# Batch 6's keys and queries turned by DMA, and divisions and roundings on any engine

## The chip, the core and the metric

The kernel runs on one core of one Trainium2 chip. The metric is device time in microseconds, from the start of the program to its end; of three runs of the kernel before, the times were 395.04, 396.47 and 396.48 us. The engines are called by the profile's names: PE (the matrix engine; PEld are its loads of stationary operands), DVE (vector), ACT (scalar), POOL (GpSimd) and SP, which here only issues DMAs.

## The reference

Attention with 16 extra "beacon" keys that every query may see, then a gated feed-forward layer without biases on the heads put side by side. B = 8 batches, H = 8 heads, S = 576 positions, D = 64; the model width is 512 and the feed-forward width 1536. Inputs and output are float32.

```python
k_all = np.concatenate([beacon_k, k], axis=2)          # 16 + 576 keys
v_all = np.concatenate([beacon_v, v], axis=2)
scores = scale * np.matmul(q, k_all.transpose(0, 1, 3, 2))
scores = np.where(causal, -1e9, scores)                # beacons are never masked
scores = scores - scores.max(-1, keepdims=True)
a = np.exp(scores)
a /= a.sum(-1, keepdims=True) + 1e-09
attn = np.matmul(a, v_all)
x = attn.transpose(0, 2, 1, 3).reshape(B * S, H * D)
out = (np.maximum(x @ w_gate, 0.0) * (x @ w_val)) @ w_out
```

## The kernel before

The work of attention goes batch by batch, and within a batch by quadruples of heads, in bf16 with sums in float32. For each batch keys and queries are loaded as float32 into staging tiles (`st`, eight of them), rounded to bf16 in `h` tiles (`rounded`, line 553; queries are scaled there) and turned over, so that the head dimension lies on the partitions: `kT` and `qT`, two buffers each. There are three ways to turn. Batches 0 to 4 use 128-wide products with an identity matrix on PE (`turned`, line 564), batches 5 and 6 the same in quadrants of 64 x 64 (`turned_pair`, line 637), each followed by a copy out of PSUM on ACT or DVE. Batch 7, which alone is in `TURN`, uses a DMA transpose (line 609) straight into `kT` and `qT`, and loads its main keys and queries in smaller pieces (line 595 in place of 598), two DMAs to a tile. Values are rounded into `v` (`copy`, lines 504 to 508).

Scores are products in quadrants on PE (line 835), into PSUM. `softmax` then works row by row of tiles of 64 to 592 elements: DVE adds the mask and finds the lowest (line 783; scores carry a minus sign), ACT takes the exponential with its sum (line 790) into `pb` or `pa` (for batch 0's first block: into a part of `xT`), DVE takes the reciprocal of the sums (line 796), and the function `norm` multiplies the tile by it in place (line 801): this is the division, always on POOL. From batch 1 or 2 on the divided weights are transposed by DMA into `pTb` and `pTa` (line 921), and before that by PE (line 911). Products with the values (line 931; 954 for the last 16 rows of all heads) give the attention's output, copied into `xT`.

The feed-forward layer works on ten spans of `xT` of 240 to 512 columns, as soon as their attention is there. For each of 12 slices of the width 1536: a gate product (line 993), ACT's relu out of PSUM (1005), a value product (999), and DVE's product of both (1010) into `hT`; then the output product (1026, 1030), a copy and a store. Weights come by DMAs that POOL issues (line 518).

`TURN`, `QUADS`, `ENG` (the engines that may round a batch's inputs) and the rest of the constants fed a planner that is no longer in the file. What it decided stands in `ORDER`, and `replay` issues it: one entry for each task, in the order in which tasks are issued, with the number of the task, a letter for the engine where it has a choice (`a` ACT, `v` DVE, `g` POOL; none: the first of the list), `w` for PE tasks that are issued in two halves of 64 columns, and after a colon the buffers taken. `f16:7` means 16 idle products on PE, which keep it at work while it would wait. Each engine works through its instructions in this order; semaphores hold an instruction until its inputs are there. PSUM's eight banks are shared: up to three for the feed-forward layer at a time.

Of the kernel before, what the change touches and what calls it, by code (L numbers as in the profile page):

```python
# [35 lines left out]
TURN = (7,)  # L36
# [6 lines left out]
ENG = [("POOL", "DVE"), ("POOL",), ("POOL",)]  # L43
# [35 lines left out]
32:2 f3:7 33a 39v:1 58:2 410:4.5.0.0 40:1 423 431:6.0 43g:2 54:1 41a 421 436 44:1 413 437 f5:7 49g:0 411 45a 412 62:7 432 415 448:3.1.0.0 47g 422 68:4  # L79
f4:7 414 449 416 70:5 451 425 51g:0 469:2.4 417 459 424 f9:7 450 426 419 470 66:6 418 460 471 14 427 452 55v:1 433 438 429 472 453 56:2 461 439 474  # L80
52:5 463 420 434 57v f2:7 435 53a 72:0 59v:2 475 73 486:5.6.0.1 63g:0 454 491 440:4 462 430 f4:7 487 464 13 64:2 455 69v 488 60:7 65v 495:3.1 428 61a
456 444:0 489 476 492 465 473 441v:0 458 445a:0 496 504:4.5 477 442:2 500 f4:7 467 77:1 443a 468 505 f4:7 501 466 513:6.0 509 17 497 f2:7 71v 522:1.2
506 81:3 514 f3:7 15 86:4 510 446:3 82 524 482:4 457 447a 515 16 507 478:3 483v:0 518 479a:0 523:5.6 18 f4:7 516 525 528 480:3 67g 484:4 519 f2:7 493
526 490 481v 557:1.2.2.3 498 485v 548:7.3 529 527 520 549 1738:0 494 553 1734:4 550 530 74:1.1 558 566:5.6 1739:1 f3:7 1735:0 562 559 499 1736:4 502
567 563 90:6 508 91 575:1.0 560 551 f2:7 554 1737:0 95:0 517 1740:2 571 125:7 568 1742:7 503 576 584:3.4 1743:2 531 1746:5 572 511 1741:1 532:7 512
586 1747:1 577 109:2 1748:5 521 580 1744:2 533a:0 552 536:1 1749:3 534:6 1745:2 78:2.1 544:5 569 537a 535v 540:2 587 561 542:1 541v:1 538:6 570 581
545v 19 585:2.3 588 543a 564 578 582 75:5 539v 1750:0 565 590 610:6.7.0 1751:1 546:4 589 555 611 591 1754:0 579 76v 1752:1 1755:0 83:0 592 612 1756:3
547v 613 1758:2 556 101:3 1753:4 594:4 1757:5 583 105:1 1759:2 614 79:7 573 596:5 595v:2 574 1762:3 593 597v 84:6 598:1 1763:1 1760:4 80a 615 602:2
599a 1761:6 606:0 600:3 92:0 603a:3 607v 87:1 616:5 604:4 85a 20 617v:0 113:4 93:0 601a 1766:1 605v 99:6 618:3 96:0 1767:2 94v 88:2 97:5 1764:4 89a
126:1.0 98v 608:7 21 619v 620:0.2.0.1 1765:7 609a 635:3.5 127:6 622 102:2 1770:7 128a 1768:4 110:1 123:3 621 1771:0 628 103:6 623 636 1772:1 129:0  # L90
1769:8 624 1774:7 643 1773:9 104a 1778:4 629 1776:0 1775:0 1779:2 1780:6 630 1777:10 1792:4 631 1781:11 644 650:7.0 1793:0 1782:1 625 637 646 626
114:2 652 639 111:4 1787:2 632 106:0 112v 638 645 633 640 115:3 651 107:6 642 659 133:1 1788 108a 116v 627 121:2 654 665:6.5 141:4 658 634 674:3.4 647
119:7 666 660 1783 649 661 670 648 667 124:1 1784 677 653 100 117:3 662 668 676 700:0.6.2.3 671 176:5 664 1794:7 708 678 655 134:1 1789 709 657 679
702 1796:5 663 1785a:0 1795:12 641 1798:3 711 680 1790v:1 122 715:7.1 710 672 656 1800:4 137:2 701 1797:0 717 130:0.0 704 1786 1802:5 1799:13 145:1
703 669 716 1804:2 1801:2 712 149:6 723 718 1806:6 681 1803:14 719 705 724 675:3.4 682 1805:1 1812w:5 118 684 690:3 726 1807:15 1808w:2 707 1813:2 683
730:6.0 725 120 1810:7 1809:1 727 732 686 729 1814:1 738 685 673 731 1816:5 1811:8 733 713 131:2 687 1815:7 1818:4 1817:1 688 739 734 1820:1 689
1819:9 741 745:3.7 735 714 720 695:1 754:5.6 740 746 1822:4 151:3 132a 737 750 1821:1 1824:0 736 747 142:0 1828:1 1823:11 1825:2 757 728 755:3.4 751
722 756 1832:2 706 1829:0 138:2 748 1826:7 752 763 758 721 1830w:0 1827:4 759 749 152 691:1 764 1833:1 693:7 1791 760 692a 1831:5 761 780:5.6.1 765
694v 135:0 762 139:1 781 1836:7 136a 146:1 770:2 742 766 782 1834:2 140v 744 783 147:4 743 143:3 767 1835:6 1838:0 1837:2 753 148v 144a 696:1 698:2
784 1839:10 785 790:5.6.0.1 805:4.7 769 786:0 798 792 768 1840:3 787a:1 699v 177:2.1 775:3 791 1841 799 794 150:0 814 788:2 793 800 807 153:0 1842 801  # L100
813 789v 820:0.5 815 795 806 773:6 1843a:2 822 808 771:2 829 1845:3 809 774v 772a 156:0 828 816 1850:6 821 160:1 810 697a 164:5 812 831 154:2 178:1
170:3 1846 797 155a 172:6 179a 835:7.4 823 1847 824 840 192:2 830 836 844:0.1 841 778:5 157:1 846 837 796 776:2 1851w 184:0 779a 847 161:2 838 825
845:4.5 1848v:0 848 188:1 1852 832 165:0 853 777a 180:7 849 826 158:7 854 166:3 839 162:0 1853v:1 1855:1 855 168:4 827 167v 174:5 811 1857:6 159a 850
817 802 1856:2 163v 852 1859:2 856 851 1858:8 870:1.0.2.3 804 857 860:2 1860:1 885:4.3 1861:6 872 834 819 842 871 1863:5 887 833 874 893 858 1862:9
873 1867:2 1864:2 169 886 894 900:6.1 889 859 1865:7 879 843 1868:0 902 895 1871:5 803 896 1866:10 193:1 888 1869:2 878 818 909 1872:1 865:1 181:2.1
881 915:7.4 908 1875:3 901 189:0 911 1870:11 171 880 182:5 916 910 1873:2 173 904 920 175 903 1879w:0 875 1876:2 1874:4 917 861:6 912 863:3 882 890
905 183v 862a 924:1.2 196:2 921 918 864v 919 925:6.7 210:1 927 1880:0 1877:5 1849 907 934 206:5 926 185:2 1881:0 202:6 1878:13 877 214:7 928 950:3.4.0
906 933 200:4 868:5 929 884 866:1 930 935 1883:2 1882:14 931 226:0 951 867a 932 190:6 186:1 1884:2 897 869v 892 1887:0 187a 952 876 953 891 194:2
1885:5 197:2 940:2 191a 954 195v 207:1 1891:4 936 203:0 937 1886:15 198:3 955 204:2 1889:6 199v 1888:2 898 1892:0 938 208:3 1895:1 1890:0 205a 227:1.0
922 209v 224:6 959:6.5.7.2.0.1 1896:1 899 1844 1899w:0 960 913 956:0 961 914 1893w:4 975 939 964 962 965 923 1897w:1 222:0 963 883 220:3 1894:1 967  # L110
1901w:6 215:0 945:1 973 1900:2 1898:2 201:1 943:4 966 976 1903w:1 944a 1902:3 980 1904w 974 223 977 941:0 986:5.3.4.6 979 942v 211:2 978 1905 989 981
999 1908:7 992 230:5 1002 997 1913:0 968 998 971 1854 985 212:2 987 957:3 1001 250:4 988 225 1909 1000 958v 221 990 213v 991 1910 218:6 983 1906a:2
238:2 970 216:5 1911v:0 1914 217a 246:7 993 994 1007:3.4.6.7 1912 969 1915w 234:0 996 1016 242:1 1008 995 946:1 948:2 1015 947a 231:2.0 1918w:5 949a
1009 251:0 1017 1105:1.2.1 219 1919 1010 1106 256:6 1011 228:6 1107 284:5 1923:3 1003 1018 229v 1108 1012 1916v:1 1920 1013 1924:0 1917 1109 1019 1004
1032:4.0.7.1.2.3 252:3 1921a:0 1110 1927:3 1033 1046 235:0 1111:1 1034 232:6 1925:2 1047 243:2 1038 1035 984 1931:5 1037 268:0 1926:4 1014 1928:1
264:4 239:1 1049 236:4 1929:2 1932:2 982 1036 233a 972 1048 1933:5 1039 1930:0 247:0 1022:0 1040 1935:6 1051 1934:6 1050 248:2 1052 240:3 244:7 1936:0
1112:5 253:1 245v 1053 1939:0 1020 1113v 241a 237v 257:2 254:6 249a 1059:1.5.3.7 1940:1 272:1 265:1 1943:4 1061 255a 1006 260:4 1071 1937:2 1005 1060
1944:2 1070 1021 1063 1054 1947:6 1938:3 1056 1027:1 1073 1064 1062 1941:4 1948:0 1041 1072 1042 1945:2 1065 269 1942:8 1074 1055 1949:1 1045 1075
1946:9 261:0 1080:3.4.5.6 1950:10 1025:2 1066 1082 1951w:7 270:6 1089 1026a 1076 1922 1088 1023:0 1079 1955w:1 1952:1 1024v 1078 1090 1081 276:7
258w:7 1069 1957w:2 1956:2 1068 1083 1953w:0 1077 1958:12 274:4 1057 1084 286:0 1959w:3 1058 1091 1954:11 1067 259a 1092 262w:1 266w:0 1093 1960:0  # L120
# [205 lines left out]
def kernel(  # L326
# [432 lines left out]
    def softmax(t, parts, ph, prio, k):  # L759
# [38 lines left out]
        for i, (n, a) in enumerate(whole):  # L798
            def norm(x, i=i, n=n, a=a):
                one = ph.tile.rearrange("p a n -> p (a n)")[:, a:a + n]  # L800
                nc.gpsimd.tensor_scalar(one, one, at(8 + i), 1.0, ALU.mult, ALU.mult)  # L801
# [315 lines left out]
```

## Time and profile before

| | |
|---|---|
| median of 3 runs | 396.47 us (395.04 to 396.48) |
| profiled execution, its own time | 395.62 us |
| its span | 393.6 us |
| busy PE / DVE / ACT / POOL | 97 / 71 / 69 / 59% of the span |
| granted PE clock | full in all 40 slices |
| DMA issues by SP: weight transposes, K/Q transposes | 34, 8 |
| divisions (line 801), all on POOL | 272, 142.4 us |
| moved by DMA | 69.0 MB, mean 175 GB/s |

The span is what the profiler saw between the first and the last instruction; the run's own time has about 2 us around it. Shares are averages over a start (to about 30 us), in which PE waits or works on idle products, a long middle in which attention and feed-forward work are interleaved, and an end of some 55 us with feed-forward work alone. Busy time of a pipelined engine counts an instruction from its start to its end, so several may overlap; start-to-start distances are the safer measure.

### The profile page before, as it was taken

What the parts mean: (1) busy time and instruction counts of PE and PEld (TensorE: products, weight loads), DVE (VectorE), ACT (ScalarE), POOL (GpSimd) and SP (SyncE); (2) the same over time, 40 slices, a digit from 0 to 9 for tenths busy, and PEclk for the clock granted to TensorE, in tenths of its full rate; (3) what the DMA queues carried; (4) which work ended last, traced back from release to release, by engine and by line L of the source; (5) the groups of instructions that cost most, each with busy time, mean ns of one, the idle gap of its engine ahead of it and who ended that gap; (6) DMA issues with size and microseconds to landing.
All of it is one profiled execution on the core that took longest, in us unless ns stands there. A gap on an engine that the chain in (4) does not pass through costs nothing.

```text
span 393.6 us, 11920 instructions
## 1 busy us (share of the span) xinstructions
PE 381.5 (97%) x4355; PEld 223.3 (57%) x4373; DVE 278.7 (71%) x1012; ACT 270.0 (69%) x838; POOL 231.4 (59%) x448
## 2 busy tenths in 40 slices
PE   7799999999999999999999999999999999999996
PEld 4457856654555456455555556555555545556664
DVE  5899899979988788888878876677838830341340
ACT  2999799897877697778893988688847723222222
POOL 3899779948796778579559584853775440000000
PEclk9999999999999999999999999999999999999999
DMA  7999999999999998998999999999896665001202
GB/s 186 229 217 228 223 215 219 188 218 218 238 223 194 294 218 192 192 249 160 208 182 263 214 207 175 220 194 163 115 210 117 108 113 163 2 0 53 84 29 93
DMA packets 184108, 69.00 MB, mean 175 GB/s; under 512 B 158385, under 2 KB 179505, under 8 KB 184049
## 3 DMA queue, kind: packets, MB, share of 16 engines
q1 hardware_dynamic: 179216, 63.46, 77.3%
q0 software_dynamic: 4752, 4.72, 7.5%
q8 instruction: 34, 0.56, 0.6%
q14 instruction: 26, 0.20, 0.2%
q10 hardware_dynamic: 80, 0.07, 0.1%
HBM read 38.54 MB, written 9.44 MB: 122 GB/s over the span
## 4 chain that ended last, share of the span: by engine, by line
PE 93%; DMA 2%; DVE 2%; SPq 1%; issue 1%; ACT 1%; POOL 0%; DVEq 0%; POOLq 0%
PE f L993 24%; PE f L999 24%; PE f L1026 22%; PE f L835 7%; PE f L931 6%; PE f L564 2%; PE f L1030 2%; PE f L911 2%; DMA st<-in_q_dram 1%; PE f L954 1%; PE f L1082 1%; PE f L885 1%; PE f L637 1%; DMA st<-in_beacon_k_dram 1%; SPq L688 0%
## 5 line engine op out<-in xcount | busy, mean ns | idle before, releaser
L801 POOL TENSOR_SCALAR pb<-pb,small 128x384 bf16<-128x384 bf16 (+8 forms) x272 | 142.4, 539 | 61.1 <-DVE small L796 45.4
L790 ACT ACTIVATE pb<-f,small 128x320 bf16<-128x320 f32 (+8 forms) x272 | 143.9, 544 | 19.6 <-DVE small L783 9.9
L783 DVE CUSTOM_DVE_ANT_0 f<-f,mask 128x448 f32<-128x448 f32 (+8 forms) x288 | 136.3, 510 | 15.5 <-PE f L835 8.9
L1010 DVE TENSOR_TENSOR hT<-g,f 128x512 bf16<-128x512 f32 (+3 forms) x120 | 74.8, 631 | 50.2 <-PE f L999 33.1
L993 PE MATMUL f<-xT,wg_r 128*64 128x512 bf16 (+5 forms) x763 | 109.5, 364 | 0.5 <-issue 0.2
L999 PE MATMUL f<-xT,wv_r 128*64 128x512 bf16 (+5 forms) x766 | 107.5, 364 | 0.3
L1026 PE MATMUL f<-wo_r,hT 128*64 128x512 bf16 (+1 forms) x717 | 94.9, 379 | 1.0 <-issue 0.5
L1005 ACT ACTIVATE g<-f 128x512 f32<-128x512 f32 (+3 forms) x120 | 65.7, 561 | 42.9 <-PE f L993 33.6
L999 PEld LDWEIGHTS <-wv_r 128*64 128x64 bf16 (+1 forms) x772 | 51.5, 107 | 37.1 <-issue 3.3
L993 PEld LDWEIGHTS <-wg_r 128*64 128x64 bf16 (+1 forms) x768 | 50.8, 107 | 38.1 <-issue 3.5
L1026 PEld LDWEIGHTS <-hT 128*64 128x64 bf16 (+1 forms) x724 | 45.5, 108 | 36.0 <-issue 1.8
L553 POOL TENSOR_SCALAR h<-st 128x512 bf16<-128x512 f32 (+1 forms) x88 | 47.7, 550 | 19.5 <-PE f L637 4.9
L790 ACT ACTIVATION_READ_ACCUMULATOR pb<-f,small 128x1 f32 x272 | 57.7, 212 | 0.0
L783 DVE DVE_READ_ACCUMULATOR2_ANT small<- 128x1 f32 x296 | 42.0, 142 | 0.0
L835 PE MATMUL f<-kT,qT 64*64 64x64 bf16 (+7 forms) x640 | 34.3, 292 | 1.6 <-ACT kT L504 0.8
L504 ACT CAST xT<-f 128x240 bf16<-128x240 f32 (+1 forms) x39 | 15.0, 391 | 22.3 <-PE f L931 22.3
L931 PEld LDWEIGHTS <-v 128*64 128x64 bf16 (+1 forms) x512 | 22.9, 109 | 9.4 <-issue 2.9
L931 PE MATMUL f<-pTb,v 128*64 128x320 bf16 (+3 forms) x488 | 28.0, 252 | 0.0
L835 PEld LDWEIGHTS <-qT 64*64 64x64 bf16 x640 | 14.9, 105 | 22.7 <-issue 18.4
L508 POOL TENSOR_SCALAR v<-st 128x512 bf16<-128x512 f32 (+1 forms) x38 | 23.3, 618 | 5.2 <-DMA st<-in_v_dram 5.1
L796 DVE RECIPROCAL small<-small 128x2 f32<-128x2 f32 (+3 forms) x136 | 19.9, 160 | 7.9 <-ACT pb L790 6.2
L504 ACT COPY osb<-f 128x512 f32<-128x512 f32 (+1 forms) x18 | 10.4, 576 | 19.7 <-PE f L1026 18.9
(66 smaller groups left out, 242.8 us busy)
## 6 DMA issues: line engine op xcount, KB each, us to landing
out_dram<-osb SPq DMA_DIRECT2D x34, 256.0 KB, 2.8
st<-in_k_dram SPq DMA_DIRECT2D x28, 256.0 KB, 4.6
st<-in_q_dram SPq DMA_DIRECT2D x28, 256.0 KB, 4.4
st<-in_v_dram SPq DMA_DIRECT2D x24, 256.0 KB, 4.3
st<-in_q_dram SPq DMA_DIRECT2D x16, 128.0 KB, 4.0
st<-in_k_dram SPq DMA_DIRECT2D x16, 128.0 KB, 3.7
st<-in_v_dram SPq DMA_DIRECT2D x8, 224.0 KB, 4.4
wv_r<-in_moe_w_val_dram POOLq DMA_DIRECT2D x3, 512.0 KB, 13.8
```

The lines of the kernel that those rows point to most:

```text
L504: nc.scalar.copy(dst, src)
L553: (nc.gpsimd if x.engine == "POOL" else nc.vector).tensor_scalar(to, src, by, 1.0, ALU.mult, ALU.mult)
L783: nc.vector.tensor_tensor_reduce(out=view(i, n - m), in0=view(i, n - m), in1=msk, scale=1.0, scalar=at(7) if m < n else 3.0e38, op0=ALU.ad ...
L790: nc.scalar.activation(ph.tile.rearrange("p a n -> p (a n)")[:, a:a + n], view(i), AF.Exp, bias=at(i), scale=-1.0, accum_out=at(4 + i))
L801: nc.gpsimd.tensor_scalar(one, one, at(8 + i), 1.0, ALU.mult, ALU.mult)
L835: nc.tensor.matmul(banks[k][b_].tile[64 * i:64 * i + 64, off:off + n], t.q.tile[r, 2 * g + i, 64 * j:64 * j + 64], t.kT.tile[r, 2 * g + i, ...
L931: nc.tensor.matmul(ps.tile[64 * hh:64 * hh + 64, d0:d0 + w], t.v.tile[:rows, c, D * h:D * h + D], rhs(64 * hh), start=(c == 0), stop=(c == ...
L993: nc.tensor.matmul(psg.tile[c:c + w, :mt], wg_r[:, ki, nf * P + c:nf * P + c + w], xT[:, ki, m0:m0 + mt], start=(ki == 0), stop=(ki == KM ...
L999: nc.tensor.matmul(psv.tile[c:c + w, :mt], wv_r[:, ki, nf * P + c:nf * P + c + w], xT[:, ki, m0:m0 + mt], start=(ki == 0), stop=(ki == KM ...
L1005: r = add("ACT", c_act(mt), lambda _, psg=psg, g=g: nc.scalar.activation(g.tile[:, :mt], psg.tile[:, :mt], AF.Relu), (a,), (psg, g), -1000 ...
L1010: hid.append(add("DVE", c_dve(mt), lambda _, psv=psv, g=g, nf=nf: nc.vector.tensor_mul(hT[nf].tile[:, :mt], g.tile[:, :mt], psv.tile[:, :m ...
L1026: nc.tensor.matmul(ps[0].tile[c:c + z, :w], hT[nf].tile[:, t0 + c:t0 + c + z], wo_r[:, nf, :w], start=(nf == 0), stop=(nf == NF - 1))
```

## The change

Batch 6 joins batch 7 in `TURN`: its keys and queries are loaded in the smaller pieces and turned by eight DMA transposes, and the 128 quadrant products on PE and eight copies out of PSUM that turned them are gone. The roundings of every batch may go to POOL, DVE or ACT (before: POOL or DVE for batch 0, POOL for the others). A division may go to POOL, ACT or DVE. The stored order is a new one: of the 272 divisions 129 stand on POOL, 72 on ACT and 71 on DVE; on PE the scores of each batch stand at about the same place in its work as before, many products are issued in full width that were issued in halves, and there are 68 idle products instead of 71.

```diff
-TURN = (7,)
+TURN = (6, 7)
...
-ENG = [("POOL", "DVE"), ("POOL",), ("POOL",)]
+ENG = [("POOL", "DVE", "ACT")] * 3
...
+NORM = ("POOL", "ACT", "DVE")
 
 ORDER = """
-12 1 22:0 10 2 26:1 9 7 2399 3 f16:7 34:3 11 8 4 30:2 0 23v:0.0 5 38:4 42:5 f1:7 27g:1.0 24:0 48:7 f3:7 25v 46:6 28:1 35v:0 29a 6 31v:2 36:3 50:0 37v
...
+10 1 22:0 8 7 2 26:1 9 2395 34:3 f16:7 4 30:2 0 5 23v:0.0 12 38:4 11 42:5 27a:1.0 24:0 48:7 f1:7 28:1 35v:0 46:6 29a 31v:2 36:3 f2:7 37v 32:2 50:3 33a
...
             def norm(x, i=i, n=n, a=a):
                 one = ph.tile.rearrange("p a n -> p (a n)")[:, a:a + n]
-                nc.gpsimd.tensor_scalar(one, one, at(8 + i), 1.0, ALU.mult, ALU.mult)
-
-            outs.append(add("POOL", c_pool(n), norm, (r,), (ph,), prio + 0.001 * i + 0.0005 * k))
+                if x.engine == "ACT":
+                    nc.scalar.activation(one, one, AF.Copy, scale=at(8 + i))
+                else:
+                    (nc.vector if x.engine == "DVE" else nc.gpsimd).tensor_scalar(one, one, at(8 + i), 1.0, ALU.mult, ALU.mult)
+
+            outs.append(add(NORM, c_pool(n), norm, (r,), (ph,), prio + 0.001 * i + 0.0005 * k))
```

Lines after the change stand 2 to 5 further down than before (line 801 is 804 on ACT and 806 on the others, 993 is 998, 609 is 611).

More of the change, by code (lines that the diff above doesn't have):

```diff
@@ L81 @@
[L81 to L120, printed above, removed]
@@ new lines @@
+911:7.4 877 904 182:5 1871:3 1866:11 185g:2 906 898 876 173g 1869:2 907 912 899 1875:0 886 900 1870:4 887g 913 183v 857:6 920:1.2 916 1876:0 202:1
+1873w:5 858a 210:7 901 908 1872:2 923 1845 921:6.7 893 917 922 196:3 859:3 220:2 888a 878 930 1877:0 879g 200:4 860a 872g 1874:13 925 873g 929
+946:3.4.0 924 880g 864:5 909g 903v 931 926 862:1 1878:14 894g 1879w:2 914 928a 863v 915g 932 865v 190w:6 1883w:0 927v 1880:2 902g 191v 203g:0 936:2
+194w:5 947 186w:1 1881w:6 195a 197g:2 933 948 949 1885w:7 935g 1882:15 934g 221a:1 910v 204w:2 187v 198w:3 1884:2 1887w:4 211g:2 950 205a 1886:0
@@ L173 @@
+2344:1 2314w 2348:2 2341w:3 2315v:2 2349w:0 2316 2326 2351w:2 2350:1 2355w:1 2346:14 2342:2 2359w:4 2361w:0 2360:2 2352:0 2357w:5 2362:4 2353w:2 2319w
+2354:15 2363w:7 2356:0 2358:3 2367w:4 2364:0 2369w:2 2368:1 2365w:0 2370:10 2371w:7 2366:8 2373w:3 2320v:1 2372:2 2321 2375w:1 2374:9 2376w 2380w:2
+2377w 2381w 2378a:0 2379 2382w 2385w:3 2383v:1 2386w 2384 2387w 2390:1.6 2388v:2 2389 2393:1 2391v:0 2394 2392
 """
```

142 lines of the change are left out of this document (88 added, 54 removed).

## The prediction, made before the changed kernel ran

> **What bounds the kernel now.** I read the page first, then the busy time by stage, then TensorE's own timeline, then the chain at the start.
>
> ```profile
> span 393.6 us, 11920 instructions
> PE 381.5 (97%) x4355; PEld 223.3 (57%) x4373; DVE 278.7 (71%) x1012; ACT 270.0 (69%) x838; POOL 231.4 (59%) x448
> ...
> PE 93%; DMA 2%; DVE 2%; SPq 1%; issue 1%; ACT 1%; POOL 0%; DVEq 0%; POOLq 0%
> ```
>
> PE is the bound, in work as in the chain that ended last. Where it rests is seen by stage; columns are busy us and instructions of PE, PEld, DVE, ACT, POOL, then the granted clock, the DMA share and GB/s:
>
> ```profile
> 0.00:20.00 20.00, 13.84 (x139) 9.64 (x140) 14.59 (x92) 12.13 (x45) 12.22 (x33) 1.00 1.00 209
> 20.00:40.00 20.00, 19.64 (x237) 13.82 (x237) 19.54 (x80) 18.79 (x54) 19.60 (x38) 1.00 1.23 222
> 40.00:60.00 20.00, 19.95 (x237) 14.45 (x235) 17.75 (x67) 16.62 (x55) 15.61 (x29) 1.00 1.09 219
> 60.00:80.00 20.00, 19.95 (x220) 12.49 (x220) 18.55 (x75) 17.94 (x61) 18.93 (x38) 1.00 1.03 205
> ...
> 380.00:394.00 14.00, 9.87 (x106) 6.55 (x100) 1.50 (x3) 2.67 (x5) 0.00 (x0) 1.00 0.20 67
> ```
>
> Of 393.6 - 381.5 = 12.1 us in which PE rests, 6.2 lie before 20 us, 0.4 in the next 20, and 13.6 - 9.9 = 3.7 at the end; about 1.8 us are left for all of 40 to 380 us. So after 40 us there is next to nothing to win from waits, and every new wait shows. What can shorten the run is less PE work, or an earlier start. At the start all three other engines are full too (19.5, 18.8 and 19.6 of 20 us).
>
> **The change on PE: quadrants against switches.**
>
> ```profile
> L637 PE MATMUL f<-ident,h 64*64 64x64 bf16 x256 | 3.5, 194 | 0.0
> L1082 PE MATMUL f<-idle 128*128 128x256 bf16 x71 | 12.1, 309 | 2.1 <-DVE idle L445 2.0 <-ACT pb L790 0.2
> ```
>
> Turning batch 6 by DMA takes 128 of the 256 quadrant products: half of 3.5 us, -1.75. Idle products go from 71 to 68; at 12.1/71 = 0.17 each at most -0.5, and since they stand where PE would wait, I take -0.3.
>
> The new order also changes how often the array is re-tiled. In PE's timeline (start, length, what, tile shape):
>
> ```profile
> 112.77 1.03 PE L999 MATMUL f<-xT,wv_r 128*128 128x512 bf16 x4
> 113.63 0.39 PE L564 MATMUL f<-ident,h 128*128 128x128 bf16 x4
> 113.85 1.03 PE L993 MATMUL f<-xT,wg_r 128*128 128x512 bf16 x4
> 114.81 0.63 PE L835 MATMUL f<-kT,qT 64*64 64x64 bf16 x16
> 115.37 1.05 PE L993 MATMUL f<-xT,wg_r 128*64 128x512 bf16 x8
> 116.26 2.11 PE L999 MATMUL f<-xT,wv_r 128*64 128x512 bf16 x18
> ```
>
> From start to start, four full products cost 0.86 us when the next group has the same shape and 0.96 when it is 64*64: a switch costs 0.10. Eight half-width products cost 0.89, as much as four full ones, so the new order's use of full width (1014 fewer rows on PE) saves nothing by itself. Going through both orders row by row I count 164 changes of tile shape before and 178 now: 14 x 0.10 = +1.4. PE's work thus moves by -1.75 - 0.3 + 1.4 = -0.65 us. The Trainium skill says in "TensorEngine Tiling (Array Packing)", section Key Properties, that changing the tiling mode drains the array; the trace's 0.10 us is the price of that here, and without it the saving would read -2.05.
>
> **The change at the start.** Two things stand differently. SP issues the second query load one place earlier, waiting for ACT's rounding instead of POOL's. Names: st are staging tiles, v is the value operand.
>
> ```order
> L660 DMA st_89<-in_k_dram 128x4x128 [waits DMAHW3_49,DVE_49]
> L660 DMA st_91<-in_k_dram 128x4x128 [waits DMAHW5_49,DMAHW4_49,DVE_49]
> L660 DMA st_90<-in_q_dram 128x4x128 [waits Pool_49]
> L660 DMA st_96<-in_q_dram 128x4x128 [waits DMAHW6_49,DMAHW0_49,Pool_49]
> L736 DMA st_93<-in_v_dram 128x8x64 [waits DMAHW7_49,DVE_49]
> ```
>
> That is before, SP's rows 12 to 16; and now:
>
> ```order
> L662 DMA st_92<-in_k_dram 128x4x128 [waits DMAHW3_49,DVE_49]
> L662 DMA st_90<-in_q_dram 128x4x128 [waits DMAHW4_49,Activation_49]
> L662 DMA st_91<-in_k_dram 128x4x128 [waits DMAHW5_49,DVE_49]
> L662 DMA st_96<-in_q_dram 128x4x128 [waits DMAHW6_49,DMAHW0_49,Pool_49]
> L738 DMA st_89<-in_v_dram 128x8x64 [waits DMAHW7_49]
> ```
>
> The query load of st_90 has moved ahead of one key load. On POOL, weight loads have moved behind the last division of xT (xT holds batch 0's first attention weights there, before the feed-forward input):
>
> ```order
> L801 TENSOR_SCALAR xT<-xT,small 128x192
> L801 TENSOR_SCALAR xT<-xT,small 128x64
> L518 DMA wg_r<-in_moe_w_gate_dram 128x4x512
> L574 MEMSET st_92 1x1
> L518 DMA wg_r<-in_moe_w_gate_dram 128x4x512
> L801 TENSOR_SCALAR xT<-xT,small 128x128
> ```
>
> And now, with four of the sixteen divisions gone to ACT and DVE:
>
> ```order
> L806 TENSOR_SCALAR xT<-xT,small 128x64
> L576 MEMSET st_96 1x1
> L806 TENSOR_SCALAR xT<-xT,small 128x128
> L806 TENSOR_SCALAR xT<-xT,small 128x256
> L520 DMA wg_r<-in_moe_w_gate_dram 128x4x512 x2
> L576 MEMSET st_92 1x1
> ```
>
> What that is worth stands in the chain at the start and in POOL's timeline:
>
> ```profile
> 7.46 1.62 SPq L660 DMA_DIRECT2D st<-in_k_dram  x2
> ...
> 9.13 5.65 DMA st<-in_q_dram
> 14.80 0.43 DVE h L553
> ...
> 26.93 0.53 PE f L993 x4
> ...
> 18.66 2.99 POOL L801 TENSOR_SCALAR xT<-xT,small 128x64 bf16<-128x64 bf16 x8
> 21.60 0.79 POOL L518 DMA_DIRECT2D wg_r<-in_moe_w_gate_dram  x1
> 22.39 0.26 POOL L574 MEMSET st<- 1x1 f32 x1
> 22.42 0.75 POOL L518 DMA_DIRECT2D wg_r<-in_moe_w_gate_dram  x1
> 23.20 0.39 POOL L801 TENSOR_SCALAR xT<-xT,small 128x128 bf16<-128x128 bf16 x1
> ```
>
> The query load lands at 14.8 us, and DVE's rounding waits for it. POOL's divisions of xT end at 23.6 us. Two weight loads (0.79 + 0.75), a memset (0.26) and four divisions (2.99/8 = 0.37 each, 1.5) leave its way: up to 3.3 us earlier. PE's first feed-forward product, at 26.93, could follow only if nothing else were late next, and ACT is: it rested 1.2 us in 20 to 40 us, and the same exponentials still stand ahead of that product. So the gain lies between 0 and 3.3; I take 0.8, what the earlier query load is worth (half of the 1.62 us that SP spent on two key loads, one of which it now overtakes: an estimate).
>
> Against it stands what ACT takes over at 30 to 40 us (g is a gate tile, whose ACTIVATE frees the PSUM bank for PE; pb and pa are attention weights being divided). Before:
>
> ```order
> L1005 ACTIVATE g_104<-f 128x240
> L790 ACTIVATE pb_76,small<-f,small 128x576
> L1005 ACTIVATE g_103<-f 128x240
> L790 ACTIVATE pa_71,small<-f,small 128x592
> L1005 ACTIVATE g_105<-f 128x240
> ```
>
> And now:
>
> ```order
> L1010 ACTIVATE g_105<-f 128x240
> L804 ACTIVATE pb_75<-pb_75,small 128x512
> L804 ACTIVATE pb_75<-pb_75,small 128x576
> L792 ACTIVATE pb_76,small<-f,small 128x576
> L1010 ACTIVATE g_103<-f 128x240
> L792 ACTIVATE pa_71,small<-f,small 128x592
> L804 ACTIVATE pb_76<-pb_76,small 128x576
> L1010 ACTIVATE g_105<-f 128x240
> ```
>
> Three large divisions stand ahead of gates that had none between them; a fourth (pa) follows. Bounds of their price come from these rows:
>
> ```profile
> L801 POOL TENSOR_SCALAR pb<-pb,small 128x384 bf16<-128x384 bf16 (+8 forms) x272 | 142.4, 539 | 61.1 <-DVE small L796 45.4
> L504 ACT CAST xT<-f 128x320 bf16<-128x320 f32 x17 | 7.2, 429 | 4.2 <-PE f L931 4.2
> L504 ACT COPY osb<-f 128x512 f32<-128x512 f32 x17 | 10.0, 589 | 18.9 <-PE f L1026 18.9
> L553 DVE TENSOR_SCALAR h<-st x8: 251/350/427, 3.9 to 16.6; 128x512 bf16<-128x512 f32 x4, 80x256 bf16<-80x256 f32 x4
> ```
>
> By ACT's copy of 512 a division of that size costs about 0.59, so four cost 2.4 us, and ACT rested 1.2 us in 20 to 40 us. The wait for PE thus lies between 0 (the rest covers it, or the copies of pTb that leave ACT soon after, four at 0.43, make up for it) and 2.4; I take what the rest does not cover, rounded down, +1.0.
>
> **The rest of the run.** Of 272 divisions 129 stay on POOL, 72 go to ACT and 71 to DVE, with 22 more roundings on DVE. ACT gains 72 x 0.43 to 0.59 = 31 to 42 us, DVE 71 x 0.25 to 0.43 + 22 x 0.43 = 27 to 40 us; POOL loses 143 x 0.54 = 77.
>
> ```profile
> 0.00:340.00 340.00, 331.67 (x3861) 190.98 (x3881) 263.87 (x988) 256.80 (x813) 231.42 (x448) 1.00 0.97 195
> ```
>
> Up to 340 us, where attention ends, DVE would work 291 to 304 of 340 us and ACT 288 to 299. On the whole that fits, so I cost it at 0; where it doesn't is rival two. Batch 6's transposes are covered as long as weight transposes land in time (rival three).
>
> Sum: -0.65 - 0.8 + 1.0 = **-0.45 us**. The profiled execution took 395.62 us (span 393.6 and 2.0 around it), 0.85 below the median of the three runs, 396.47; taken from the median, 396.47 - 0.45 gives **396.0 us**.
>
> **Rivals.** *One, the start gives more:* ACT is not in the way, and POOL's 3.3 us reach PE. For it speaks that POOL was busy 19.6 of 20 us; against it, ACT's 18.8. Time: 396.47 - 0.65 - 3.3 = 392.5.
>
> *Two, slower: DVE becomes late.* In 20 to 80 us DVE rested only 0.5 + 2.25 + 1.45 = 4.2 us, and up to the 24th feed-forward product on it (near 76 us) the new order gives it 9 divisions and 2 more roundings, 11 x 0.25 to 0.43 = 2.8 to 4.7 us. It decides from where that passes the rest. The trace also shows DVE and POOL holding each other up:
>
> ```profile
> 16.59 0.42 DVE L553 TENSOR_SCALAR h<-st 128x512 bf16<-128x512 f32 x1
> ...
> 18.06 0.79 DVE L506 CAST v<-st 128x512 bf16<-128x512 f32 x1
> ...
> 16.66 0.37 POOL L574 MEMSET st<- 1x1 f32 x1
> ...
> 17.83 0.79 POOL L518 DMA_DIRECT2D wg_r<-in_moe_w_gate_dram  x1
> ...
> 28.85 0.09 POOL L574 MEMSET st<- 1x1 f32 x1
> ```
>
> The same memset took 0.09 us at 28.85 and 0.37 beside DVE's rounding of h at 16.59; a DVE rounding of 512 took 0.79 beside POOL's weight load of 17.83, and 0.42 otherwise: up to 0.37 each. There are 93 more such DVE instructions; if POOL works 45% of the time (231.4 - 77 us of 340), that is 93 x 0.45 x 0.37 = 15 us of DVE at most; if 4.5 us of it fall where DVE has no rest, the time is 396.0 + 4.5 = 400.5 us. The Trainium skill states the rule in "SBUF — State Buffer", section Who interferes with whom: a VectorE copy, cast or tensor_scalar in a two-port mode and a GpSimd instruction exclude each other for the whole instruction. By that rule the 0.37 and the 0.79 are such waits; the trace agrees.
>
> *Three, slower: SP's queue at batch 6.*
>
> ```profile
> L609 SPq DMA_TRANSPOSE kT<-h x4: 1227/1301/1787, 253.3 to 281.7; - x4
> L595 SPq DMA_DIRECT2D st<-in_q_dram x8: 432/505/575, 233.9 to 273.3; - x8
> ...
> DMA to landing us min/median/max: 2.9/6.3/8.4
> ...
> 201.42 3.78 SPq L921 DMA_TRANSPOSE pTb<-pb  x1
> ...
> 209.13 0.81 PE f L931 x16
> ```
>
> Eight transposes at 1.3 and eight more loads at 0.5 add 14.4 us to SP within some 50 us. A weight transpose, issued at 201.42, is used by PE at 209.13, 7.7 us later, and such transposes land after 6.3 (median) to 8.4 us. So a delay above 1.4 us shows; I price it at +3: 399.5 us.
>
> **How the numbers follow.** A measurement of this kernel tells 0.5%, 2 us, from no change. My forecast, within that, 0.45; rival one 0.20 (faster); rivals two and three 0.27 and 0.08 (slower, 0.35). The range takes in both outer rivals with half a microsecond beyond each, 392.0 to 401.0, and leaves out what lies further out than their prices; the forecast's own is 394.6 to 398.4.
>
> **What would show it.** Right: PE's busy sum near 381, quadrants (L639) at half of 3.5 us, PE resting under 3 us between 40 and 380 us, and the first gate product between 25.5 and 27 us. Rival one: that product by 24. Rival two: waits of PE for DVE or ACT in 30 to 100 us, and divisions on DVE above 0.43. Rival three: PE waiting for pTb near 205 to 260 us. It is wrong altogether if PE's work per product or its clock (1.00 in every stage shown) changes.

## The result and the profile after

The changed kernel takes 399.42 us (median of 10 runs, 397.12 to 401.28) against 395.75 us (10 runs, 394.81 to 397.42): a ratio of 1.009, interval 1.0069 to 1.0111, or 3.7 us more. The forecast was 396.0, no change. The profiled execution took 399.30 us, its span 397.6.

The page, first busy time by engine and then the chain that ended last:

```profile
span 397.6 us, 10895 instructions
...
PE 383.5 (96%) x3833; PEld 210.1 (53%) x3866; DVE 299.2 (75%) x1099; ACT 299.9 (75%) x923; POOL 140.2 (35%) x268
...
PE 62%; ACT 15%; DVE 8%; DMA 5%; issue 4%; SPq 3%; POOL 1%; DVEq 0%; ACTq 0%; POOLq 0%
```

PE is still busy for 96% of the span, but the chain runs over it for 62% only (93% before): the rest goes through ACT, DVE and a DMA. ACT and DVE have gained 30 and 20 us, POOL has lost 91. By stage (columns as before):

```profile
0.00:20.00 20.00, 15.60 (x151) 10.27 (x151) 15.31 (x97) 12.71 (x47) 10.48 (x28) 0.91 0.96 207
20.00:40.00 20.00, 18.33 (x223) 13.10 (x220) 19.27 (x78) 19.61 (x57) 17.14 (x33) 1.00 1.19 217
...
0.00:340.00 340.00, 329.59 (x3301) 180.04 (x3336) 281.36 (x1071) 286.06 (x898) 140.21 (x268) 0.99 0.98 198
```

Where the time goes is seen best at a landmark that both orders put at nearly the same place of PE's work: the scores of a batch's last 16 rows (eight products of 128 x 32). In PE's timeline they start, for batches 0, 5 and 7, here:

```profile
36.59 0.44 PE L885 MATMUL f<-kT,qT 128*32 128x512 bf16 x8
...
204.81 0.43 PE L885 MATMUL f<-kT,qT 128*32 128x512 bf16 x8
...
297.04 0.43 PE L885 MATMUL f<-kT,qT 128*32 128x512 bf16 x8
```

That was before. And now:

```profile
36.52 0.44 PE L890 MATMUL f<-kT,qT 128*32 128x512 bf16 x8
...
206.53 0.43 PE L890 MATMUL f<-kT,qT 128*32 128x512 bf16 x8
...
300.76 0.44 PE L890 MATMUL f<-kT,qT 128*32 128x512 bf16 x8
```

In these two profiles the start is a draw. From batch 0 to batch 5 it is 168.2 us before and 170.0 now, from batch 5 to batch 7 92.2 and 94.2. So two losses, 1.8 and 2.0 us, one spread over the middle and one around batches 6 and 7.

The second has one large row, in the waits of PE:

```profile
PE f L936 <- DMA pTb<-pb: 1.0, 1, 1.0
```

The first has none; its waits are of 0.1 to 0.3 us. They sit in part inside what counts as busy, as an experiment below shows.

### The profile page after: what moved, and what is told of

It reads as the page before. It is cut to its first block, busy times and chain, and to the rows that moved or that the text cites. A ratio compares the mean times of both kernels' runs of the same rounds, so it can differ in the third digit from the quotient of the medians.

```text
span 397.6 us, 10895 instructions
## 1 busy us (share of the span) xinstructions
PE 383.5 (96%) x3833; PEld 210.1 (53%) x3866; DVE 299.2 (75%) x1099; ACT 299.9 (75%) x923; POOL 140.2 (35%) x268
## 4 chain that ended last, share of the span: by engine, by line
PE 62%; ACT 15%; DVE 8%; DMA 5%; issue 4%; SPq 3%; POOL 1%; DVEq 0%; ACTq 0%; POOLq 0%
PE f L1004 18%; PE f L998 17%; PE f L1031 15%; ACT pb L792 8%; PE f L840 4%; PE f L936 3%; DVE f L785 3%; PE f L566 2%; DMA pTb<-pb 2%; ACT g L1010 2%; DMA kT<-h 1%; ACT pb L804 1%; SPq L926 1%; DMA st<-in_q_dram 1%; DVE hT L1015 1%
## 5 line engine op out<-in xcount | busy, mean ns | idle before, releaser
L792 ACT ACTIVATE pb<-f,small 128x448 bf16<-128x448 f32 (+8 forms) x272 | 145.5, 558 | 13.8 <-DVE small L785 8.2
L785 DVE CUSTOM_DVE_ANT_0 f<-f,mask 128x576 f32<-128x576 f32 (+8 forms) x288 | 136.4, 507 | 13.4 <-PE f L840 9.9
L806 POOL TENSOR_SCALAR pb<-pb,small 128x448 bf16<-128x448 bf16 (+8 forms) x140 | 76.8, 560 | 94.0 <-DVE small L798 79.9
L998 PEld LDWEIGHTS <-wg_r 128*64 128x64 bf16 (+1 forms) x660 | 48.6, 104 | 42.5 <-issue 4.1
L1004 PEld LDWEIGHTS <-wv_r 128*128 128x128 bf16 (+1 forms) x644 | 47.6, 104 | 42.6 <-issue 4.7
L792 ACT ACTIVATION_READ_ACCUMULATOR pb<-f,small 128x1 f32 x272 | 62.2, 229 | 0.0
L1031 PEld LDWEIGHTS <-hT 128*64 128x64 bf16 (+1 forms) x580 | 40.3, 105 | 40.5 <-issue 2.0
L555 POOL TENSOR_SCALAR h<-st 128x512 bf16<-128x512 f32 (+1 forms) x65 | 35.0, 546 | 71.0 <-issue 21.7
L804 ACT ACTIVATE pb<-pb,small 128x384 bf16<-128x384 bf16 (+8 forms) x67 | 34.3, 548 | 1.1 <-DVE small L798 0.9
L506 ACT CAST xT<-f 128x240 bf16<-128x240 f32 (+2 forms) x51 | 18.7, 387 | 16.1 <-PE f L936 15.4
```

The costliest lines, as they stand in the source:

```text
L555: (nc.gpsimd if x.engine == "POOL" else nc.vector).tensor_scalar(to, src, by, 1.0, ALU.mult, ALU.mult)
L785: nc.vector.tensor_tensor_reduce(out=view(i, n - m), in0=view(i, n - m), in1=msk, scale=1.0, scalar=at(7) if m < n else 3.0e38, op0=ALU.ad ...
L792: nc.scalar.activation(ph.tile.rearrange("p a n -> p (a n)")[:, a:a + n], view(i), AF.Exp, bias=at(i), scale=-1.0, accum_out=at(4 + i))
L804: nc.scalar.activation(one, one, AF.Copy, scale=at(8 + i))
L806: (nc.vector if x.engine == "DVE" else nc.gpsimd).tensor_scalar(one, one, at(8 + i), 1.0, ALU.mult, ALU.mult)
L998: nc.tensor.matmul(psg.tile[c:c + w, :mt], wg_r[:, ki, nf * P + c:nf * P + c + w], xT[:, ki, m0:m0 + mt], start=(ki == 0), stop=(ki == KM ...
```

## The experiments

Each run is set against the kernel before on the same chip. The table has the medians, the ratio of the means, and the two distances just read, from batch 0's last-rows scores to batch 5's (middle) and from there to batch 7's (late), in the run's one profile. Where two runs have the same work in a stretch, its length repeats closely (from batch 0 to batch 1: 37.91, 37.92 and 37.91 us in the changed kernel, no_turn6 and after_h7). The medians are less sharp: a difference between two rows of the table carries about 1 us either way.

| run | us | before | ratio (interval) | middle | late |
|---|---|---|---|---|---|
| the kernel before | 395.75 | | | 168.2 | 92.2 |
| the changed kernel | 399.42 | 395.75 | 1.0090 (1.0069 to 1.0111) | 170.0 | 94.2 |
| no_act_div | 397.56 | 395.49 | 1.0055 (1.0035 to 1.0076) | 169.0 | 95.0 |
| no_dve_div | 399.14 | 395.49 | 1.0089 (1.0074 to 1.0105) | 169.6 | 93.8 |
| no_div | 398.33 | 396.18 | 1.0049 (1.0031 to 1.0068) | 169.2 | 95.1 |
| no_pool_div | 401.62 | 395.49 | 1.0153 (1.0138 to 1.0167) | 171.1 | 96.0 |
| no_turn6 | 397.96 | 395.49 | 1.0059 (1.0046 to 1.0072) | 170.1 | 92.7 |
| no_act_turn6 | 396.15 | 396.03 | 0.9998 (0.9987 to 1.0010) | 168.9 | 93.6 |
| no_dve_turn6 | 397.57 | 396.03 | 1.0040 (1.0022 to 1.0058) | 169.7 | 92.7 |
| no_div_turn6 | 395.38 | 396.29 | 0.9987 (0.9965 to 1.0009) | 168.4 | 92.6 |
| before_no143 | 396.08 | 396.18 | 0.9998 (0.9985 to 1.0011) | 168.4 | 92.2 |
| after_modes | 400.61 | 396.29 | 1.0114 (1.0084 to 1.0143) | 171.6 | 94.2 |
| after_h7 | 399.62 | 396.29 | 1.0084 (1.0058 to 1.0109) | 170.1 | 94.7 |
| after_modes_h7 | 400.63 | 396.29 | 1.0109 (1.0083 to 1.0136) | 171.5 | 94.0 |
| after_h7_sp | 401.95 | 396.18 | 1.0143 (1.0109 to 1.0176) | 170.3 | 94.5 |
| act_to_pool | 406.69 | 396.18 | 1.0273 (1.0230 to 1.0317) | 176.3 | 96.6 |
| after_norm_pool | 409.74 | 396.03 | 1.0355 (1.0324 to 1.0386) | 176.7 | 95.0 |
| after_quad6 | 404.32 | 396.03 | 1.0211 (1.0194 to 1.0229) | 170.8 | 98.7 |
| before_norm_any | 405.74 | 396.03 | 1.0251 (1.0231 to 1.0271) | 177.6 | 92.8 |
| before_dma6 | 410.74 | 396.03 | 1.0374 (1.0356 to 1.0393) | 168.2 | 107.0 |

**Undoing or doing one part.** The first four runs take one part out of the changed kernel, or put one into the kernel before.

after_norm_pool, where the letter behind the number of each division is dropped in ORDER:

```diff
-1400a 354g:1
+1400 354g:1
```

> The changed kernel with all 296 divisions back on POOL; its order, its roundings and the DMA turn of batch 6 stay. To explain are 3.7 us (399.4 against 395.75). If divisions on ACT and DVE make those two late (rival two), 2 to 3 of them come back: 396.5 to 397.5 us, PE's residual waits between 45 and 112 us fall from 2.7 to about 1.7, and the wait for pTb near 253 us stays. If the cost is the batch 6 turn, the time stays at 399 to 400. If it is the order itself, which was laid out with divisions spread over three engines, POOL is late in places and the time rises above 400.

after_quad6, with the quadrant products set in where two adjoining PSUM banks are free:

```diff
-TURN = (6, 7)
+TURN = (7,)
```

> The changed kernel with batch 6 turned in quadrants on PE again (eight DMA transposes and the split loads gone, 128 quadrant products and eight copies on ACT and DVE back), all else as changed. PE has 1.75 us more to do. If SP's queue and the transfers of batch 6 are the cost (rival three), the waits between 235 and 330 us (about 2.2 us more than before) go and the time is 1.75 - 2.2, about 399.0, or 398 if more hangs on them. If divisions are the cost, it rises by 1.5 to 2, to 401.

before_norm_any, the kernel before with the changed `norm` and the changed kernel's letters on its divisions:

```diff
-            outs.append(add("POOL", c_pool(n), norm, (r,), (ph,), prio + 0.001 * i + 0.0005 * k))
+            outs.append(add(("POOL", "ACT", "DVE"), c_pool(n), norm, (r,), (ph,), prio + 0.001 * i + 0.0005 * k))
```

> The kernel before with each division on the engine that the changed kernel gives it (153 POOL, 72 ACT, 71 DVE), each at its place in the old order; nothing else changed. If divisions on ACT and DVE are the cost: plus 2 to 3 us, 398 to 399. If the batch 6 turn or the new order is: within 1 us of 395.75; POOL's relief may even show as a gain of up to 1 us.

before_dma6, in the kernel before:

```diff
-TURN = (7,)
+TURN = (6, 7)
```

> The kernel before with batch 6 in TURN: its keys and queries loaded in two pieces and turned by eight DMA transposes, each issued 12 places after its rounding; 128 quadrant products and eight copies gone; nothing else changed. Without harm from SP it gains 1.75 us: 394.0. If SP's queue and transfers near batch 6 are the cost (rival three): 395.5 to 397.5, with PE waiting for pTb or kT between 200 and 300 us.

All four came out slower than the kernel they started from: by 10.0 us over the changed kernel, 4.6 over it, 9.7 over the kernel before, and 14.7. Only one case of one expectation, that the order was laid out for its engines, covers what came. The waits say why: in before_dma6, PE waits for batch 7's roundings on POOL, which stand behind work that the old order did not plan for.

```profile
PE f L563 <- POOL h L552: 6.5, 2, 4.8
PE f L930 <- DMA pTb<-pb: 2.8, 2, 2.6
```

A long wait is paid for twice here. Behind the one of 4.81 us in before_dma6 the granted clock averages 0.52 from 262 to 268 us (the third column from the end); in after_norm_pool it is 0.50 from 107 to 110 us, behind a wait of 3.76.

```profile
262.00:268.00 6.00, 5.18 (x38) 2.08 (x39) 0.33 (x1) 2.37 (x9) 5.67 (x11) 0.52 0.99 239
```

A stored order fits one placement of the work. A part that is undone within it measures the misfit, several times the size of what is looked for. They tell one thing: the parts that the forecast took as nearly free cost 10 to 15 us when the order is not laid out for them. So the next runs move nothing; they leave out.

**Leaving out.** In `norm`, here for ACT, and in the transposes of batch 6:

```diff
+                if x.engine == "ACT":
+                    return
...
-lambda _: nc.sync.dma_start_transpose(
+lambda _: b != 6 and nc.sync.dma_start_transpose(
```

> The changed kernel without the 72 divisions that stand on ACT (left out, so 38 us of ACT's work are gone and the weights of those tiles stay undivided). If ACT, made late by divisions, holds PE back (rival two, on ACT rather than DVE), PE's small waits between 36 and 200 us, 2.0 to 2.5 us more than before, mostly go and so do those on ACT near 27 us (1.1) and 297 to 305 us (0.8): 396 to 397 us. If the waits belong to DVE or to the order, it gains under 1 us: 398.5 or more. 399.4 is the time to compare with.

> The changed kernel without the 71 divisions that stand on DVE (22 us of its work). If DVE, late or locked with POOL, is what holds PE back (rival two as it was put): 396.5 to 397.5 us, with PE's small waits between 36 and 200 us down by 1.5 to 2. If ACT is: under 1 us gained.

> The changed kernel without the 153 divisions left on POOL (83 us of its work). POOL works 35% of the time now, so by all theories but one it gains under 0.5 us beside what the weight transposes win by being issued earlier near 240 to 255 us (up to 1.2). If POOL and DVE holding each other up is the cost, the gain is 1.5 us or more, spread over 36 to 320 us, and DVE's divisions take less than their 0.325 us.

> The changed kernel with batch 6's eight DMA transposes left out (kT and qT of that batch keep old data there), its split loads, roundings and all else kept: 10 us of SP's issuing gone between 225 and 300 us. If SP's queue at batch 6 and 7 is a cost (rival three), the wait for pTb at 254 us (1.0) and the waits of 0.2 to 0.4 at 275 to 305 us go: 397.3 to 398.2 us. If these waits come from late exponentials and divisions instead, under 0.5 us.

ACT's divisions gave 1.6 us, batch 6's transposes 1.2, DVE's nothing, each give or take about 1. By the table, ACT's give 1.0 us in the middle and lose 0.8 late; the transposes give nothing in the middle and 1.6 late. (The profile of no_act_div is also 0.6 us ahead at batch 0, but 0.5 of that by 15.4 us, before the first division on ACT at 18.5.) SP's timeline shows how the transposes cost. In the changed kernel, ahead of the weight transpose for which PE waits:

```profile
237.45 2.24 SPq L611 DMA_TRANSPOSE qT<-h  x1
239.74 1.28 SPq L690 DMA_DIRECT2D st<-in_q_dram  x2
241.07 1.21 SPq L611 DMA_TRANSPOSE kT<-h  x1
242.38 3.82 SPq L926 DMA_TRANSPOSE pTb<-pb  x1
246.25 0.58 SPq L1049 DMA_DIRECT2D out_dram<-osb  x1
246.88 4.05 SPq L926 DMA_TRANSPOSE pTb<-pb  x1
```

And without batch 6's transposes:

```profile
234.87 1.27 SPq L690 DMA_DIRECT2D st<-in_q_dram  x2
238.91 3.79 SPq L926 DMA_TRANSPOSE pTb<-pb  x1
242.75 0.58 SPq L1049 DMA_DIRECT2D out_dram<-osb  x1
243.38 4.22 SPq L926 DMA_TRANSPOSE pTb<-pb  x1
```

From 236 to 251 us SP has no pause any more, and the last of these is issued at 246.88 instead of 243.38. PE in the changed kernel, where 16 products of weights and values wait for it:

```profile
253.30 0.71 PE L936 MATMUL f<-pTb,v 128*64 128x320 bf16 x10
255.04 0.88 PE L936 MATMUL f<-pTb,v 128*64 128x320 bf16 x16 [1.02 <-DMA pTb<-pb]
```

In no_pool_div the surprise is the sign: 83 us less work on POOL and 2.5 us slower than the changed kernel. POOL issues four weight loads 5 us earlier, at 16.27 to 19.29 us instead of 21.43 to 24.44; and the chain that ended last now holds one row that has no like in the changed kernel:

```profile
25.60 15.45 DMA st<-in_q_dram
```

A load of queries that lands after 15.45 us (median 4.6 in this run) delays a rounding and what stands behind it, and PE rests 1.4 of the 10 us from 40 to 50 us (0.15 in the changed kernel). That the earlier weight loads made it slow fits, but no run isolates it; and 1.7 us more than in the changed kernel are lost late, where PE waits for pTb (2.1 us in all). The prices on DVE did not move:

```profile
L808 DVE TENSOR_SCALAR pb<-pb,small 128x384 bf16<-128x384 bf16 (+8 forms) x65 | 19.7, 321 | 0.2
```

against 20.0 us and 325 ns in the changed kernel. So divisions on DVE and divisions on POOL holding each other up is not the cost.

**Both at once, and a control.** no_div leaves out the 143 divisions on ACT and DVE, no_div_turn6 these and the transposes; before_no143 leaves the same 143 out of the kernel before.

> The changed kernel with the 72 divisions on ACT, the 71 on DVE and batch 6's eight DMA transposes left out (those weights stay undivided, batch 6's kT and qT keep old data). Alone the three gave 1.6, 0 and 1.2 us of the 3.7. If these are separate costs that add up: 396.5. If what is left is the order's own (14 more changes of shape, 1.3 us), the time stays there and does not reach the kernel before. If they overlap (each only hides the other's waits), it stays above 397.

> The changed kernel without the 143 divisions on ACT and DVE, batch 6's transposes kept. With these left out as well it ran 0.9 us under the kernel before, 4.5 us under the changed one; alone ACT's gave 1.6, DVE's 0 and the transposes 1.2. If ACT and DVE share one cost (either being late is enough): about 396.5, that is 3.3 of the 4.5. If the costs are separate: 397.8, and the surplus of the joint run came from the transposes.

> The kernel before without the same 143 divisions, which all stand on POOL there (77 us of its work): a control for the runs that leave work out. If less work on engines beside PE wins time in any version of this kernel, it gains 1 us or more, and the gains of the other runs say nothing of the change. If the old order has next to nothing to win from waits after 40 us: within 0.5 us of 395.75, or slower, as leaving out POOL's divisions made the changed kernel 2.4 us slower by letting weight loads start earlier beside the loads of keys and queries.

no_div_turn6 is 0.9 us under the kernel before, not told from it. The control moves by 0.1: leaving out these divisions wins nothing in the kernel before, so what it wins here belongs to the change. (There they relieve POOL; what relieving ACT or DVE would win in the kernel before was not run.) The sum does not add up: 1.5 us without the divisions, 1.2 without the transposes, 4.6 without both, a surplus of 1.9 (1.2 by the means) that alone is hardly clear of the intervals. The table says where it would come from. Without the divisions the middle is 0.8 us shorter and the late part 0.9 longer: PE is at the late wait sooner and waits longer there, since what ends it is SP's queue: the transpose that it waits for is issued at 246.82 us in no_div and at 246.88 in the changed kernel. The waits for pTb in no_div (1.0 in the changed kernel):

```profile
PE f L938 <- DMA pTb<-pb: 1.8, 2, 1.1
```

The page of no_div_turn6, with as many PE records as the changed kernel's (x3833) of the same PE program:

```profile
PE 380.4 (97%) x3833; PEld 208.3 (53%) x3866; DVE 284.2 (72%) x1028; ACT 273.2 (70%) x851; POOL 139.6 (36%) x268
```

So the changed kernel's 383.5 us are not all work. Of the 3.1 us between them 0.4 lie in the first 20 us, where the granted clock was 0.91 against 1.00; the rest is best read as time in which a group that has started waits.

With the late wait at 254 us out of the way, one engine's divisions at a time:

> The changed kernel without ACT's 72 divisions and without batch 6's eight DMA transposes; DVE keeps its 71 divisions. Against the kernel before, the transposes' absence alone leaves 2.5 us, and with both engines' divisions left out -0.9. If the wait for pTb near 254 us had only hidden what ACT's divisions cost: -0.9 to 0. If DVE's divisions cost as much, which alone they did not show: plus 0.8 or more.

> The same with DVE's 71 divisions left out and ACT's 72 kept. If only ACT's cost time: plus 2.0 to 2.5 against the kernel before, as without the transposes alone. If DVE's cost was hidden by the wait near 254 us: plus 1.5 or less.

Against no_turn6 (2.5 us over the kernel before), leaving out ACT's gives 2.4 us and DVE's 0.9. Together 3.3, and both left out gave 3.4: now it adds up, within intervals of 0.7 to 0.9 us on each. The landmarks bear ACT's part out. Batch 6's scores, with ACT's divisions (no_turn6) and without them (no_act_turn6):

```profile
255.59 0.44 PE L890 MATMUL f<-kT,qT 128*32 128x512 bf16 x8
...
253.38 0.44 PE L892 MATMUL f<-kT,qT 128*32 128x512 bf16 x8
```

That is 2.2 us, 0.45 of it from the start. It comes in small steps, the same in both pairs of runs that differ in ACT's divisions alone: 0.47 and 0.49 us from batch 0 to batch 1, 0.44 and 0.45 from batch 3 to batch 4. In no_act_turn6 a later wait for pTb, of 1.37 us at 271.9, then takes most of it back in this profile. DVE's divisions show 0.4 us in the middle by the table. A division that is left out relieves its engine and also lets the transpose behind it start sooner; the runs don't part the two.

**What did not mend it.** after_modes changes only the choice of full width or halves, so that the array is re-tiled 156 times instead of 178; after_h7 gives batch 6 four more `h` tiles; after_modes_h7 has both; after_h7_sp has the tiles and moves two weight transposes (tasks 1401 and 1406) ahead of a key transpose (352); act_to_pool moves ACT's divisions to POOL. One line of each, in this order:

```diff
-1792w:5
+1792:5
...
-cast_s = Slots(many(3, [P, DM], BF16, "h16"))
+cast_s = Slots(many(3, [P, DM], BF16, "h16") + [xT[:, i, NT - S:NT - S + DM] for i in range(KM)])
...
-1373g 352
+1373g 1401:2 1406:3 352
...
-1400a 354g:1
+1400g 354g:1
```

> The changed kernel with only the choice between full width and two halves set anew for 64 of its products, so that the array changes its tile shape 156 times instead of 178 (before: 164); order, engines and buffers stay. If a change of shape costs 0.095 us wherever it stands, 22 fewer give 2.1 us: 397.3. If PE waits elsewhere soon after in any case, or half-width products are dearer than the rows of 0.86 and 0.89 say: 399 or more.

> The changed kernel with four more h tiles for batch 6's eight roundings of keys and queries (they lie in the part of xT that batch 7 fills later), nothing else changed. In the changed profile POOL's roundings waited for DMA transposes to let go of one of three h tiles (0.6 and 4.7 us near 236 and 239 us), with divisions of pb, and behind them the transpose of pb that PE waited for at 254, queued behind on POOL. If this is how batch 6 costs, the 1.0 to 1.4 us that go without its transposes go here too: 398.0 to 398.4. If it is SP's time to issue them: no gain, 399 or more.

> Both of these together. If both theories hold and add up: 399.4 - 2.1 - 1.2 = 396.1, within 0.5 us of the kernel before. If only the shapes count 397.3, if only the tiles 398.2, if neither 399.4.

> The changed kernel with the four more h tiles, and with two weight transposes (the ones that ran at 242.4 and 246.9 us) moved ahead of one of batch 6's key transposes and of a store in SP's order, all else kept. With the tiles alone the wait for pTb at 254 us stayed at 1.0 us, SP being without a pause from 226 to 262. If SP's order there is the cost, the wait goes: 398.4 or less, against 399.4 to 399.6. If PE then waits for that key transpose instead: 399.5.

> The changed kernel with its 72 divisions on ACT moved to POOL at the same places of the order (complete: no work left out); DVE keeps its 71, batch 6 its transposes. POOL works 35% of the time and would work about 46%. If ACT being late costs 1.6 us and POOL has room where they stand: 397.8 to 398.3. If POOL is not free at those places (all 143 on POOL gave 10 us more), it comes out above 400.

None gained. after_modes took 22 changes of shape away and is 0.6 us further over the kernel before than the changed kernel is, which its interval doesn't tell from none; its middle is 1.6 us longer, and the loss stands between batch 2's scores and batch 4's (54.9 us against 52.9). Why is not settled: its chain there runs over loads and roundings of queries. after_modes_h7 came out as after_modes did. after_h7 differs by 0.3 us, inside its interval: PE still waits 1.0 us for pTb, and SP still issues without a pause. The missing `h` tiles were not the cost. after_h7_sp is 2.1 us slower than the changed kernel; the wait for pTb is gone and PE waits elsewhere:

```profile
PE f L1031 <- ACT osb L506: 1.6, 1, 1.6
```

act_to_pool is 10.5 us over the kernel before, though POOL works only 43% of its span: PE waits 3.6 us in all for weight transposes, and once 3.3 us for DVE.

```profile
PE f L936 <- DMA pTb<-pb: 3.6, 3, 1.4
PE f L840 <- DVE hT L1015: 3.3, 1, 3.3
```

Most of the loss has one place: from batch 1's last-rows scores to batch 2's it is 40.9 us, against 34.2 in the changed kernel. The long wait stands there, and behind it the granted clock is 0.50 for six microseconds; four full products, 0.86 us from start to start elsewhere, take 1.70 from 106.24 us on. So the clock adds nearly 3 us to the wait.

```profile
103.03 0.64 PE L840 MATMUL f<-kT,qT 64*64 64x192 bf16 x8 [3.32 <-DVE hT L1015]
...
106.24 1.91 PE L998 MATMUL f<-xT,wg_r 128*128 128x512 bf16 x4
107.94 1.70 PE L1004 MATMUL f<-xT,wv_r 128*128 128x512 bf16 x4
...
103.00:109.00 6.00, 5.97 (x27) 2.07 (x27) 4.10 (x16) 5.13 (x18) 2.12 (x4) 0.50 1.07 224
```

No run points to a version that beats both kernels.

## Why the prediction was wrong

**The failed step is "On the whole that fits, so I cost it at 0".** It held 11 to 15% of rest over 340 us against the new work and found room. The busy sums came a little below the forecast (DVE 281 of 340 against 291 to 304, ACT 286 against 288 to 299), so there was room on average. But leaving that work out, with the wait at 254 us gone, gives 2.4 us for ACT's divisions and 0.9 for DVE's. An average rest did not cover 72 delays of 0.55 us on the engine that also frees PE's banks; that it is the banks is argued, not shown. The count was off as well: there are 296 divisions, so 153 and not 129 stay on POOL; the 143 that leave it were right. And the sum for ACT leaves out 15 roundings that moved to it (9 of keys and queries, 6 of values, 8.4 us); they also stand in no_div_turn6, which is level with the kernel before.

**Batch 6 was covered "as long as weight transposes land in time"; they didn't.** Rival three named the queue, the place (a wait for pTb between 205 and 260 us) and a price of 3 us. The place was right to the wait at 254 us. Its price is 1.2 us with the divisions in place, and 3.1 without them (from no_div's 2.2 us over the kernel before to no_div_turn6's 0.9 under it; 2.5 by the means and in the late column). Its chance of 0.08 looks too low: a delay above 1.4 us was to show, and the transpose that PE waits for is issued 3.5 us later than without batch 6's. That its time, 399.5, is 0.1 from the measured one is luck: it put 3 us on this queue, which with all else in place gives 1.2 of the loss of 3.7.

**Rival two had the right kind of cost on the wrong engine.** DVE's divisions cost 0.325 us each, within 0.25 to 0.43, and POOL's divisions do not hold them up: without POOL's they take 321 ns. The Trainium skill's rule that was weighed there ("SBUF — State Buffer", section Who interferes with whom) had explained two rows of the start; over 65 divisions beside POOL's, this measurement shows 4 ns, so next to nothing of the loss comes from there. ACT was the larger part:

```profile
L804 ACT ACTIVATE pb<-pb,small 128x384 bf16<-128x384 bf16 (+8 forms) x67 | 34.3, 548 | 1.1 <-DVE small L798 0.9
...
L806 DVE TENSOR_SCALAR pb<-pb,small 128x384 bf16<-128x384 bf16 (+8 forms) x65 | 20.0, 325 | 0.2
```

**PE's term held where it can be read.** The quadrants went as said, 1.75 of 3.5 us:

```profile
L639 PE MATMUL f<-ident,h 64*64 64x64 bf16 x128 | 1.7, 194 | 0.0
```

PE's work, -0.65 by the sum, can't be read from busy sums: a page can lack records (no_div_turn6's has 3833 of the 3866 products that no_turn6's has of the same PE program), and the kernel before and its control, with equal records and times, read 381.5 and 383.1. For the same reason the sign of under 3 us of rest between 40 and 380 us (4.3 in the profile) says little. no_div_turn6, 0.9 us under the kernel before with an interval from 1.4 under to 0.4 over, agrees with -0.65 and does not show it. The 14 changes of shape at 0.10 could not be tested: taking 22 away moved nothing to the better.

**Both terms of the start are there, smaller, and a slower clock beside them.** The first gate product stands at 26.38 us (25.5 to 27 forecast, 26.87 before), and what is late next is ACT, as said:

```profile
26.38 0.58 PE L998 MATMUL f<-xT,wg_r 128*128 128x240 bf16 x4
27.77 0.57 PE L998 MATMUL f<-xT,wg_r 128*128 128x240 bf16 x4 [0.80 <-ACT pb L792]
```

The divisions on ACT at 37 to 42 us, which were to cost 1.0, took more than the 0.59 that a copy's row had given:

```profile
36.95 1.40 ACT L804 ACTIVATE pb<-pb,small 128x512 bf16<-128x512 bf16 x2
...
40.27 0.76 ACT L804 ACTIVATE pb<-pb,small 128x576 bf16<-128x576 bf16 x1
...
41.18 0.78 ACT L804 ACTIVATE pa<-pa,small 128x592 bf16<-128x592 bf16 x1
```

That price falls behind batch 0's scores at 36.5 us, and is read from there to batch 1's: 37.91 us in the changed kernel, 37.43 without ACT's divisions. Of the +1.0, 0.5 came. (Before it was 37.02; the other 0.4 is in the new order, and no run says where.)

The gain of 0.8 is seen where the granted clock stays at 1.00 for the first 20 us, as in the profile before. Of the changed kernel and the fifteen runs made from it, six have that in their profiles, and batch 0's scores stand at 35.59 to 36.34 us there, 36.59 before. In the other ten, the changed kernel's among them, the clock falls to between 0.51 and 0.81 from 10 to 15 us, and they stand at 36.14 to 37.22. So the draw of 36.52 against 36.59 reads as a gain of some 0.7 us and a slower clock that takes it back. That the clock might change was among the signs of being wrong; here it is worth less than 1 us. It fits that no_act_div (35.94) and no_div_turn6 (35.69) look faster at the start: both have the full clock. Rival one (a gain of 3.3) did not occur.

What is settled: the loss comes with ACT's divisions (2.4 us, give or take 0.7) and with SP's queue at batch 6, which hides most of what relieving the others gives. DVE's divisions (0.9) are at the edge of what the intervals tell apart. What is open: whether ACT's divisions cost by holding up PE's banks, which the chain over ACT suggests, or by their own length ahead of the transposes; and why fewer changes of shape made the middle longer.

## What to carry to other kernels

Room in an average does not pay for work on an engine that frees the bound engine's buffers: price such work by each place where it stands ahead of a release. Two waits in series on different resources can overlap; take one away and the other grows, so leave out both before calling either small. In a kernel with a stored order, leave work out to measure a part of a change, with the same work left out of the kernel before as a control; moving work measures the order's misfit. Look at the granted clock behind every long wait before pricing it.

## What the runs showed of the hardware

A PE wait of some microseconds cost more than its length: behind 3.32 us (act_to_pool), 3.76 (after_norm_pool) and 4.81 (before_dma6) the granted clock was 0.50 for about 6, 3 and 6 us, and in the first two runs four full products took 1.70 us from start to start instead of 0.86. Behind the changed kernel's wait of 1.02 us for pTb it stayed at 1.00.

At the start the clock fell in ten of the sixteen profiles named above and stayed full in six; a wait of 0.9 to 1.1 us near 7.6 us stands in all of them, so it doesn't decide this alone. The fall came although PE issued idle products in that time. In the changed kernel:

```profile
10.00:15.00 5.00, 4.38 (x38) 2.38 (x35) 4.47 (x32) 4.20 (x21) 2.77 (x4) 0.66 1.13 264
```

Less work on POOL made the kernel slower by 2.5 us: weight loads were issued 5 us earlier, and one load of queries took 15.45 us to land where the median is 4.6 (that the one caused the other is not shown). And a busy PE hid waits, up to 2.7 us in the changed kernel.
